# The last two output tiles stored whole, one by ScalarE and one by SP

## The chip, the cores and the metric

The kernel runs on one core of one Trainium2 chip. The metric is the device time of one execution in microseconds (us), as the median of several runs. A profiled execution comes with a trace: its span runs from the first to the last instruction, and all times in the rows below are microseconds from the start of that span. In the rows PE is TensorE (PEld its weight loads), DVE is VectorE, ACT is ScalarE, POOL is GpSimd and SP is SyncE. A "q" behind an engine's name (SPq, ACTq) is its instruction queue: the issue of a transfer, a branch or a wait.

## The reference, cut to what matters

The first half is a gated linear attention (an mLSTM) over 4 batches, 8 heads, 768 steps and 40 values per head. Its output, reordered to 3072 tokens of 320 values, goes through a feed-forward layer of width 2048 with a rational activation:

```python
x = attn_out.transpose(0, 2, 1, 3).reshape(B * S, H * D)   # 3072 x 320
h = x @ w_in
P = a[0] + a[1] * h + a[2] * h**2 + a[3] * h**3
Q = 1.0 + abs(b[0]) * abs(h) + abs(b[1]) * h**2
out = (P / (Q + 1e-06)) @ w_out                            # 3072 x 320
```

The change concerns how the last rows of `out` leave the chip, and nothing of the computation.

## The kernel before, in words

A flag computed at the start selects one of two copies of the whole program (`tc.If` and `Else`); the profiled execution ran the first. Behind the selected copy each engine takes a branch (line 328) past the other copy, to a common ending (line 1479) in which SP waits for the transfers' semaphores and the engines meet.

The attention produces token blocks; the feed-forward layer takes them in 12 steps of 256 tokens, numbered 0 to 11. Each step has eight chunks of the hidden width and collects its result in two PSUM tiles of 128 tokens by 320 values, `po`. At its end the operation `ev` (`f_ev`) copies each of them to an SBUF tile, `ot` (128 partitions of 320 float32, 160 KB), and `ed` (`f_ed`) stores it to `out`. The 128 partitions of a tile are 64 steps of one batch and the same 64 steps of the next batch, and the batches lie 768 rows apart in `out`. So a store of the first kind writes 64 partitions (80 KB) to 64 consecutive rows, and a tile takes two such stores.

All engine work stands in one list, `ORDER`, written out by hand; the operations are recorded in that order, and each engine keeps it. In it `ed` is an operation on SP for all tiles but the very last. The last step, 11, has the tiles `ot11_0` and `ot11_1`. ScalarE evicts the first and VectorE the second, at about the same time. The two stores of `ot11_0` are issued by SP (operation `ed_11_7`). The two stores of `ot11_1` are issued from inside `f_ev`, the first by ScalarE's queue and the second by SP:

```python
if engine == "DVE" and not split:
    f_ed(t, (nc.scalar, nc.sync))
```

As line 30 (`_Queue`) hands out `dma_start` of any queue but SP's unwrapped, ScalarE's store carries its own line number (L1360) in the trace, and those of SP carry that of the helper, L34.

Of the kernel before, what the change touches and what calls it, by code (L numbers as in the profile page):

```python
# [314 lines left out]
whalf_11_7.1 m_11_6 rm_11_6 gl_11_5 p1half_11_7.1 p3half_11_7.1 f3_11_4 f3_11_4.1 f2_11_5 f2_11_5.1 yhalf_11_7  # L315
r0half_11_7 ghhalf_11_7 mhalf_11_7 rmhalf_11_7 f3_11_5 f3_11_5.1 f2_11_6 f2_11_6.1 gl_11_6 f3_11_6 f3_11_6.1
yhalf_11_7.1 r0half_11_7.1 ghhalf_11_7.1 mhalf_11_7.1 rmhalf_11_7.1 glhalf_11_7 glhalf_11_7.1 f2half_11_7
f2half_11_7.1 f3half_11_7 f3half_11_7.1 ev_11_7 ed_11_7 ev_11_7.1
"""


# [69 lines left out]
def _program(  # L391
# [16 lines left out]
    nc = _Ordered(tc)  # L408
    B, H, S, D = q.shape
    DM, DFF = w_in.shape  # L410
    P = 128
    L = 64
# [47 lines left out]
    def ring(pool, tag, shape, name, dt=F32, at=None):  # L460
        k = plan.slot[tag] if at is None else at
        return pool.tile(shape, dt, tag=f"{tag}{k}", name=name, bufs=1)
# [759 lines left out]
    def feed_forward(n, i):  # L1222
        d = {}
        size = SIZES[n]
        split = n < SPLIT
# [3 lines left out]
        last = n == len(SIZES) - 1 and i >= NS - HALVED  # L1229
# [77 lines left out]
        def parts_of(t):  # L1307
            return [(t, 0, 0, DM)] if t < 8 - BANKS else [(0, DM, 0, 512 - DM), (1, DM, 512 - DM, DM)]
# [28 lines left out]
        def f_ev(t, engine):  # L1337
            ot = d["ot", t] = ring(fp, "ot", [P, DM], f"ot{n}_{t}")
            for b, at, lo, hi in parts_of(t):
                to, po = ot[:, lo:hi], PO[n, half][b][:, at : at + hi - lo]  # L1340
                if split:
                    nc.vector.scalar_tensor_tensor(
                        to, po, pa[:, 3:4] if square else 1.0, PT[n][:, t, lo:hi], op0=ALU.mult, op1=ALU.add
                    )
                elif engine == "DVE":
                    nc.vector.tensor_scalar(to, po, pa[:, 3:4] if square else 1.0, None, op0=ALU.mult)
                elif square:
                    nc.scalar.activation(to, po, AF.Copy, scale=pa[:, 3:4])
                else:
                    nc.scalar.copy(to, po)  # L1350
            if engine == "DVE" and not split:
                f_ed(t, (nc.scalar, nc.sync))

        def f_ed(t, queues):
            m = firsts_of[n] + t // 2
            blk, b = divmod(2 * m, B)
            at = blk * P + t % 2 * L
            for j, queue in enumerate(queues):
                rows = out.rearrange("(b s) e -> b s e", b=B)[b + j, at : at + L]
                queue.dma_start(rows, d["ot", t][j * L : (j + 1) * L])  # L1360

        k = f"{n}_{i}"
        a0, a1 = (ps[:, 0:1], ps[:, 1:2]) if square else (pa[:, 0:1], pa[:, 1:2])
# [1 line left out]
        def add(name, engine, cost, fn, r=(), w=(), new=(), part=None, **kw):  # L1365

            def own(x):
                if x not in ("h", "ha", "w", "p", "gH", "gL"):
                    return x
                if part is None or not last:  # L1370
                    return f"{x}{k}"
                return f"h{k}p{part}" if x == "h" else f"{x}{k}.{part}"

            plan.add(
                f"{name}{'half' if last and part is not None else ''}_{k}", engine, cost, fn,
                [own(x) for x in r], [*(own(x) for x in w), f"turn {name}"],
                [(own(x).split(".")[0], t) for x, t in new], **kw,
            )
# [39 lines left out]
        if i == NS - 1:  # L1418
            for t in range(groups):
                o = f"ot{n}_{t}"  # L1420
                e = "DVE" if split or t == groups - 1 and n == len(SIZES) - 1 else "ACT"
                add("ev", e, 0.32, lambda t=t, e=e: f_ev(t, e), r=[f"pt{n}.{t}"] if split else [],
                    w=[*(po[b] for b, *_ in parts_of(t)), o], new=[(o, ("ot", BUFS["ot"]))], lag=2.5)
                if e == "ACT" or split:
                    add("ed", "SP", 0.6, lambda t=t: f_ed(t, (nc.sync, nc.sync)), r=[o], lag=2.5)

    stg = ctx.enter_context(tc.tile_pool(name="stage", bufs=2))
# [18 lines left out]
    for n, i in steps + [(n, i) for n in range(SPLIT, len(SIZES)) for i in range(NS)]:  # L1446
        feed_forward(n, i)
# [36 lines left out]
```

## Time and profile before

| | |
|---|---|
| device time, 3 runs | 499.54, 499.55 and 501.44 us; median 499.55 us |
| the profiled execution's own time | 500.97 us |
| its span, first to last instruction | 499.1 us |
| what lies outside the span | 1.9 us |
| mean granted TensorE clock | 0.993 |
| TensorE busy | 479.0 us (96% of the span) |
| last matmul ends, last eviction ends | 491.5 us, 492.1 us |

The profiled execution is 1.4 us above the median of the runs, so differences worked out on the span are laid on the median. The change is confined to what follows 491.9 us: the last 7 us of the span, in which no engine computes.

### The profile page before, as it was taken

How to read it: one execution, taken by the hardware profiler on the slowest of the kernel's cores; microseconds unless marked ns; L12 is line 12 of the kernel's file. 1: busy time of each engine (PE TensorE's matmuls, PEld its weight loads, DVE VectorE, ACT ScalarE, POOL GpSimd, SP SyncE). 2: the span in 40 equal slices, each digit the busy share in tenths (PEclk: the TensorE clock that was granted, in tenths of full speed). 3: DMA queues.
4: the chain of work that ended last, by engine and by line, in shares of the span. 5: the costliest groups of instructions: out<-in, count | busy, mean ns of one | idle time of the engine just before them, and what ended most of it. 6: DMA issues, size and time to landing. Idle time of an engine off the chain costs nothing.

```text
span 499.1 us, 14216 instructions
## 1 busy us (share of the span) xinstructions
PE 479.0 (96%) x5631; PEld 460.3 (92%) x5631; DVE 415.7 (83%) x696; ACT 402.6 (81%) x701; POOL 394.6 (79%) x392
## 2 busy tenths in 40 slices
PE   4899999999999999999999999999999999999993
PEld 4789989899999999999999999999999999999993
DVE  6789899999889788997788977888887788868793
ACT  1779999879977587879886888997778788778981
POOL 3789899888796888888889787888677877887772
PEclk9999999999999999999999999999999999999998
DMA  7979965157444343731541330504241040010101
GB/s 195 230 149 250 303 148 106 36 97 139 102 88 87 73 73 62 150 83 24 100 101 43 67 72 1 110 1 102 65 107 18 2 88 1 1 30 2 26 1 34
DMA packets 119837, 42.01 MB, mean 84 GB/s; under 512 B 104274, under 2 KB 112530, under 8 KB 119762
## 3 DMA queue, kind: packets, MB, share of 16 engines
q1 hardware_dynamic: 118626, 40.77, 37.4%
q8 instruction: 46, 0.75, 0.7%
q10 hardware_dynamic: 1136, 0.25, 0.3%
q14 instruction: 29, 0.24, 0.2%
HBM read 36.90 MB, written 4.10 MB: 82 GB/s over the span
## 4 chain that ended last, share of the span: by engine, by line
PE 75%; DVE 7%; POOL 4%; ACT 4%; issue 3%; DMA 1%; POOLq 0%; DVEq 0%
PE ph L34 31%; PE po L34 29%; PE y L34 4%; PE kq L34 4%; PE ow L34 3%; PE ps L34 2%; DVE w L34 2%; DMA qn<-in_q_dram 1%; PE px L34 1%; DVE gH L34 1%; PE hot L34 1%; POOL p L34 1%; DVE gL L34 1%; POOL w L34 1%; POOL wi L34 1%
## 5 line engine op out<-in xcount | busy, mean ns | idle before, releaser
L34 POOL TENSOR_TENSOR p<-p,w 128x512 f32<-128x512 f32 (+1 forms) x97 | 131.1, 1352 | 61.1 <-DVE w L34 58.3
L34 PE MATMUL ph<-xk,wi 128*128 128x256 f32 x1152 | 169.4, 283 | 1.7 <-DVE xk L34 0.8
L34 PEld LDWEIGHTS ph<-xk,wi 128*128 128x128 f32 x1152 | 148.1, 188 | 3.9 <-DVE xk L34 1.0
L34 PE MATMUL po<-wo,gH 128*128 128x320 f32 x768 | 133.4, 310 | 0.0
L34 POOL TENSOR_TENSOR w<-w,ha 128x512 f32<-128x512 f32 (+1 forms) x97 | 127.1, 1313 | 6.4 <-ACT w L34 3.2
L34 PEld LDWEIGHTS po<-wo,gH 128*128 128x128 f32 x768 | 115.6, 188 | 0.7
L34 DVE SCALAR_TENSOR_TENSOR gL<-p,ps,ph 128x512 fp32r<-128x512 f32 (+1 forms) x97 | 71.1, 734 | 21.5 <-POOL p L34 19.8
L34 DVE SCALAR_TENSOR_TENSOR w<-w,gH 128x512 f32<-128x512 f32 (+1 forms) x97 | 83.9, 865 | 3.9
L34 ACT ACTIVATE ph<-w,cd 128x512 f32<-128x512 f32 (+1 forms) x97 | 66.5, 686 | 21.4 <-DVE p L34 11.0
L34 ACT ACTIVATE w<-ha,ba 128x512 f32<-128x512 f32 (+1 forms) x97 | 78.6, 811 | 5.5 <-POOL p L34 2.1
L34 DVE SCALAR_TENSOR_TENSOR gH<-p,ps,ph 128x512 fp32r<-128x512 f32 (+1 forms) x97 | 71.4, 736 | 13.3 <-ACT ph L34 7.4
L34 PE MATMUL po<-wo,gL 128*128 128x320 f32 x384 | 77.2, 314 | 0.8 <-DVE gL L34 0.6
L34 PE MATMUL ph<-xk,wj 128*128 128x256 f32 x384 | 75.2, 277 | 0.0
L34 DVE SCALAR_TENSOR_TENSOR p<-p,ps,ph 128x512 f32<-128x512 f32 (+1 forms) x97 | 70.2, 732 | 4.7 <-ACT p L34 3.6
L34 ACT ACTIVATE ha<-ph 128x512 f32<-128x512 f32 (+1 forms) x97 | 57.3, 591 | 15.5 <-PE ph L34 15.1
L34 ACT ACTIVATE p<-ph,ps 128x512 f32<-128x512 f32 (+1 forms) x97 | 65.3, 678 | 4.1 <-DVE gL L34 3.6
L34 PEld LDWEIGHTS po<-wo,gL 128*128 128x128 f32 x384 | 59.0, 188 | 3.1 <-DVE gL L34 2.3
L34 PEld LDWEIGHTS ph<-xk,wj 128*128 128x128 f32 x384 | 58.0, 188 | 0.0
L34 ACT ACTIVATE ph<-ph 128x512 f32<-128x512 f32 (+1 forms) x97 | 56.0, 578 | 2.1
L34 PE MATMUL hot<-ident 128*128 128x128 f32 x180 | 25.6, 293 | 4.0 <-DVE flag_out L386 4.0
L34 PEld LDWEIGHTS hot<-ident 128*128 128x128 f32 x180 | 23.3, 205 | 4.5 <-issue 4.0
L34 DVE TENSOR_TENSOR pm<-ps,e 128x256 f32<-128x256 f32 x48 | 18.6, 418 | 9.1 <-PE ps L34 8.8
(133 smaller groups left out, 605.7 us busy)
## 6 DMA issues: line engine op xcount, KB each, us to landing
rawo<-in_moe_w_out_dram SPq DMA_DIRECT2D x8, 640.0 KB, 7.7
ab<-scrA SPq DMA_DIRECT2D x40, 128.0 KB, 3.4
rawi<-in_moe_w_in_dram SPq DMA_DIRECT2D x8, 512.0 KB, 6.7
kr<-in_k_dram SPq DMA_DIRECT2D x24, 160.0 KB, 3.5
qn<-in_q_dram SPq DMA_DIRECT2D x24, 160.0 KB, 3.6
og<-in_o_gate_dram SPq DMA_DIRECT2D x48, 80.0 KB, 3.3
out_dram<-ot SPq DMA_DIRECT2D x47, 80.0 KB, 2.3
vb<-in_v_dram SPq DMA_DIRECT2D x46, 80.0 KB, 3.1
```

Of the source, the lines that this page charges most:

```text
L34: made = fn(*args, **kwargs)
```

## The change

The two stores of each of the last two tiles become one store of 128 partitions. Its destination is an access pattern of three levels: 2 batches, 64 rows in each, 320 values. ScalarE's queue issues that of `ot11_0`, which it evicted itself, and SP that of `ot11_1`, which VectorE evicted. Both are issued from inside `f_ev`, so the operation `ed_11_7` leaves the list. All other tiles are stored as before.

```diff
@@ ORDER, its end
-f2half_11_7.1 f3half_11_7 f3half_11_7.1 ev_11_7 ed_11_7 ev_11_7.1
+f2half_11_7.1 f3half_11_7 f3half_11_7.1 ev_11_7 ev_11_7.1
@@ f_ev
-            if engine == "DVE" and not split:
-                f_ed(t, (nc.scalar, nc.sync))
+            if last and not split:
+                f_ed(t, (nc.scalar if engine == "ACT" else nc.sync,))
@@ f_ed
-            for j, queue in enumerate(queues):
-                rows = out.rearrange("(b s) e -> b s e", b=B)[b + j, at : at + L]
-                queue.dma_start(rows, d["ot", t][j * L : (j + 1) * L])
+            rows = out.rearrange("(b s) e -> b s e", b=B)[b : b + 2, at : at + L]
+            if len(queues) == 1:
+                queues[0].dma_start(rows, d["ot", t])
+            else:
+                for j, queue in enumerate(queues):
+                    queue.dma_start(rows[j], d["ot", t][j * L : (j + 1) * L])
@@ feed_forward
-                if e == "ACT" or split:
+                if split or not last:
                     add("ed", "SP", 0.6, lambda t=t: f_ed(t, (nc.sync, nc.sync)), r=[o], lag=2.5)
```

SP's instructions at the end of the executed copy, before the change; a row names the destination, the source, the destination's shape from the slowest level to the fastest, and the semaphores waited for (DMAHW is that of an earlier transfer):

```order
L34 DMA out_dram<-ot_1_7407 64x320 [waits DMAHW0_49,Activation_49]
L34 DMA out_dram<-ot_1_7407 64x320 [waits DMAHW1_49]
L34 DMA out_dram<-ot_0_7673 64x320 [waits DMAHW2_49,Activation_49]
L34 DMA out_dram<-ot_0_7673 64x320 [waits DMAHW4_49]
L34 DMA out_dram<-ot_1_7677 64x320 [waits DMAHW5_49,DVE_49]
L328 UNCONDITIONAL_BRANCH
```

The same place after it:

```order
L34 DMA out_dram<-ot_1_7407 64x320 [waits DMAHW0_49,Activation_49]
L34 DMA out_dram<-ot_1_7407 64x320 [waits DMAHW1_49]
L34 DMA out_dram<-ot_1_7676 2x64x320 [waits DMAHW3_49,DVE_49]
L328 UNCONDITIONAL_BRANCH
```

Three stores of 64x320 have become one of 2x64x320, which waits for VectorE's eviction; the stores of step 10 above it stand as they did.

ScalarE's last instructions before the change:

```order
L34 ACTIVATE ph_7_1_7589<-ph_7_1_7589 128x256 [waits Activation_49]
L34 ACTIVATE ot_0_7673<-po_0_0_7419,pa 128x320 [waits DMAHW7_49,DMAHW6_49,PE_49]
L1360 DMA out_dram<-ot_1_7677 64x320 [waits DVE_49]
L328 UNCONDITIONAL_BRANCH
```

And after it:

```order
L34 ACTIVATE ph_7_1_7589<-ph_7_1_7589 128x256 [waits Activation_49]
L34 ACTIVATE ot_0_7673<-po_0_0_7419,pa 128x320 [waits DMAHW7_49,DMAHW6_49,PE_49]
L1360 DMA out_dram<-ot_0_7673 2x64x320 [waits Activation_49]
L328 UNCONDITIONAL_BRANCH
```

ScalarE still issues one store; it now waits for its own eviction in place of VectorE's. No other row of any engine has moved, in either copy of the program.

## Rows read from the trace of the kernel before

**Rows 1.** The page: span, and busy time of the engines.
```profile
span 499.1 us, 14216 instructions
PE 479.0 (96%) x5631; PEld 460.3 (92%) x5631; DVE 415.7 (83%) x696; ACT 402.6 (81%) x701; POOL 394.6 (79%) x392
```

**Rows 2.** The timeline from 491.3 us to the end: start, duration, instruction.
```profile
490.94 0.57 PE L34 MATMUL po<-wo,gL 128*128 128x320 f32 x2
491.40 0.53 ACT L34 ACTIVATE ot<-po,pa 128x320 f32<-128x320 f32 x1 [3.45 <-PE po L34]
491.55 0.55 DVE L34 TENSOR_SCALAR ot<-po,pa 128x320 f32<-128x320 f32 x1 [0.66 <-PE po L34]
491.95 2.60 SPq L34 DMA_DIRECT2D out_dram<-ot  x3
492.13 0.55 ACTq L1360 DMA_DIRECT2D out_dram<-ot  x1
```

**Rows 3.** SP's three last issues, apart: duration in ns, and time to landing.
```profile
L34 SPq DMA_DIRECT2D out_dram<-ot x1: 467/467/467, 492.0 to 492.0; - x1
DMA to landing us min/median/max: 2.6/2.6/2.6
...
L34 SPq DMA_DIRECT2D out_dram<-ot x1: 1348/1348/1348, 492.5 to 492.5; - x1
DMA to landing us min/median/max: 2.9/2.9/2.9
...
L34 SPq DMA_DIRECT2D out_dram<-ot x1: 637/637/637, 493.9 to 493.9; - x1
DMA to landing us min/median/max: 3.7/3.7/3.7
```

**Rows 4.** The branch to the ending: duration in ns, first and last start.
```profile
L328 ACTq COMPARE_BRANCH  x1: 38/38/38, 492.7 to 492.7; - x1
L328 SPq COMPARE_BRANCH  x1: 46/46/46, 494.6 to 494.6; - x1
```

**Rows 5.** The ending itself, columns as before; the last row of 497.9 to 498.2 us.
```profile
L1479 SPq EVENT_SEMAPHORE  x10: 17/28/28, 497.7 to 499.0; - x10
L1479 DVEq DRAIN  x2: 10/26/41, 495.1 to 498.6; - x2
L1479 ACTq DRAIN  x2: 8/38/67, 495.6 to 498.6; - x2
...
L1479 SPq EVENT_SEMAPHORE  x6: 28/28/28, 497.9 to 498.2; - x6
```

**Rows 6.** Transfers, 492 to 499.1 us: busy tenths of 16 engines in 40 slices.
```profile
DMA  0002108979720179158960010010000000000100
```

**Rows 7.** Queues, 495.06 to 496.51 us, then 496.49 to 497.06: packets, MB, share.
```profile
q8 instruction: 1, 0.02, 6.2%
...
DMA  6000000006000000006000000000600000000000
q1 hardware_dynamic: 5, 0.01, 6.7%
```

**Rows 8.** Transfers, 1.6 to 1.7 us, and the first issue of the span.
```profile
q1 hardware_dynamic: 2, 0.00, 1.0%
...
flag_a<-in_moe_a_dram SPq DMA_DIRECT2D x1, 0.0 KB
```

**Rows 9.** Transfers, 494.08 to 494.26 us: the rest of ScalarE's store.
```profile
DMA packets 7, 0.01 MB, mean 43 GB/s; under 512 B 1, under 2 KB 7, under 8 KB 7
q10 hardware_dynamic: 7, 0.01, 11.9%
```

**Rows 10.** Transfers, 468 to 472 us: four stores of step 10.
```profile
DMA packets 320, 0.33 MB, mean 82 GB/s; under 512 B 64, under 2 KB 320, under 8 KB 320
q1 hardware_dynamic: 320, 0.33, 38.2%
```

## The prediction, made before the changed kernel ran

> **What bounds the kernel now.** The page comes first: TensorE is busy 96% of a span of 499.1 us [rows 1]. The change touches nothing before 491.9 us, so only the end matters. The timeline shows that the two evictions end at 491.93 (ScalarE) and 492.10 (VectorE), and that nothing but four issues of stores follows [rows 2]. Yet the span goes on for 7.0 us, and the views of single lines tell with what.
>
> SP issues three stores one after another: 0.47, 1.35 and 0.64 us long, the last from 493.91 to 494.55 [rows 3]. Then it branches at 494.6 [rows 4], and its first instruction in the ending starts at 497.7, 3.1 us later [rows 5]. ScalarE's way is alike: branch at 492.7, ending at 495.6. So a jump costs an engine about 3 us here, and SP jumps last. From SP's first wait in the ending to the end of the span it is another 1.4 us [rows 5].
>
> The last store lands 3.7 us after 493.91, at 497.6 [rows 3], just before SP begins to wait. That is late by its own measure: its last engine sent four packets between 496.5 and 497.04, when the rest was done, and right before them a block of 16 KB of instructions had held one engine: 6.2% of 16 engines over 1.45 us, so 1.4 us [rows 7]. Two things thus end almost together: SP's own way (issue, jump, waits), which decides, and the landing of the last store, just ahead of SP's first wait.
>
> **The change, part by part.** One store costs an issuer one issue whatever its rows, if the issues behind these rows are a guide: the four here move the same 80 KB in 0.47 to 1.35 us. I take 0.55 us, ScalarE's [rows 2]; 1.35, met where SP and ScalarE issued together, is the other end.
>
> *SP's way.* Two of its three issues go. Its one store waits for VectorE's eviction, as ScalarE's did, and so starts at 492.13 [rows 2]. It ends between 492.6 and 493.5, in place of 494.55: SP reaches its jump 1.05 to 1.95 us earlier, and its first wait at 495.8 to 496.7. Nothing is queued behind this issue but the jump.
>
> *ScalarE's way.* Its store waits for its own eviction and starts at 491.95, when SP's first did. Its jump comes 0.2 us earlier, which gains nothing: it was in the ending 2 us ahead of SP [rows 5].
>
> *The transfers.* This is where the sum is decided: the bytes are the same, 256 rows of 1280 bytes, but over how many of the 16 engines? A store of 64 rows leaves 80 packets: 64 rows, and 16 small ones that report completion, one for each engine (four stores: 320 packets, 64 of them under 512 bytes [rows 10]). The one transfer in the program whose slowest level is 1, the flag's single row, leaves 2 packets, one of data and one of completion [rows 8]: it used one engine. So the shape decides the count. Every other transfer here has 16 or a multiple of 16 as its slowest level on both sides; the new stores are the first with a slowest level of 2, by the order's rows (2x64x320). I take it that the slowest level is what is dealt out, and that each new store runs on two engines, 64 rows on each. The trace has no transfer with a 2 in that place, so this is inference between two ends: 2 engines, or 16 as for the stores before.
>
> The Trainium skill states the rule by which this would happen, in "DMA: Bandwidth & Descriptors", section "Why a DMA increments its semaphore by 16 and not by 1": the engines of a transfer are the largest number up to 16 that divides the slowest level other than 1 on both sides, and they are the lowest-numbered ones. For 128 partitions against 2 batches it gives 2, and the same two for both stores. The trace agrees as far as its single-row transfer goes (one completion packet); no run so far shows a 2.
>
> *The price on two engines.* If both stores are dealt out from the same first engine, each of the two has 128 rows to send. For a row's price the nearest stretch is the one in which two late engines alone finish ScalarE's store: 7 packets, one of them small, in 11.9% of 16 engines over 0.18 us [rows 9], 0.34 us for 6 rows, or 57 ns a row. The other ends are 95 ns with all 16 engines at work (38.2% of 16 engines over 4 us for 256 rows [rows 10]) and some 140 ns for the last engine after the block of instructions (four rows in 0.55 us [rows 7]). Two engines that are otherwise alone are the case of the first. 128 x 57 ns is 7.3 us. That both take the same pair is a choice too: no row tells which engine is which, but nothing in the two issues differs that could part them. Separate pairs are priced with the rivals.
>
> *The sum.* ScalarE's issue ends at 492.50; after SP's first issue ended at 492.42 the first packets of stores came with the seventh of the 40 slices, from 493.07 on, 0.65 us later (the digits before it are instructions) [rows 6]. So packets run from 493.15 to 500.45. A last packet reported 0.5 us after it left (497.04 to 497.6 [rows 3, 7]): 500.95. SP has been waiting since 496.7 at the latest; when its wait for these stores is released, the rest of its list and the ending remain, 1.2 us by the row from 497.9 to the end [rows 5] (1.0 to 1.4). The span ends at 502.15, 3.05 us later than before. The gain on SP's way is swallowed whole: it is 4 us ahead of the landing. On the profiled execution that is 504.0 us, on the median 499.55 + 3.05 = **502.6 us**.
>
> **The rivals.**
>
> *Sixteen engines, so faster.* If rows are dealt out by their total, 128, each engine has 16 rows for both stores: at 95 ns that is 1.5 us, and all has landed by 495.4 even if SP's issue takes 1.35 us. SP first asks at 495.8. Then its shorter way is the whole result: 1.05 to 1.95 us less, 497.6 to 498.5 us. For it speaks that every store so far used 16 engines; against it, that all of those had a slowest level of 64. The point from which it decides: what lands by 497.9 costs nothing against before, so an engine may spend 4.2 us on its rows, 74 of them at 57 ns. 256 rows need at least four engines for that.
>
> The Trainium skill also advises this very step, in "DMA: Bandwidth & Descriptors", section "Rules for kernel authors": two transfers to disjoint halves of the partitions gain nothing, and one of 128 partitions is to be used. By that alone the result would be this rival's. Its reason is that both halves use all 16 engines anyway, which rows 10 agree with for the stores of before.
>
> *Two engines at the loaded price, so slower by more.* Two queues would feed the same two engines, which no stretch of the trace shows. At 95 ns, 128 rows take 12.2 us, and the time is 499.55 + 8.0 = 507.5 us; at 140 ns it is 513. For it speaks that single late engine; against it the stretch of rows 9, where two late engines were quick.
>
> *Two engines, and a block of instructions on one of them.* Every jump fetches instructions over the same 16 engines. A block that falls on one of the two adds up to its 1.4 us: 504.0 us. Of the four last stores ScalarE's [rows 9] and SP's last [rows 7] ended on late engines, so this is no rarity.
>
> *Two separate pairs, so no change.* With 64 rows an engine, 3.65 us from 493.3 to 494.1 on, the later store lands between 497.5 and 498.3 and the span ends 1.2 us behind that: 0.4 us less to 0.4 us more, 499.1 to 500.0 us. Rows 9 fit it as well as they fit one pair.
>
> **How the numbers follow.** One pair near 57 ns a row gets 0.52, one pair at a higher price or behind instructions 0.23, sixteen engines (or at least four a store) 0.20, two pairs 0.05. The prediction is the first: 502.6 us, by itself 502.0 to 506.0 with the dearer rows and the fetched blocks counted in. The range for all has to reach into the sixteen-engine case, 497.6 to 498.5; from 497.8 to 505.5 it leaves out a little of that case and about half of the dear one, some 0.17. Half a per cent, 2.5 us, is about what a measurement here tells from no change. Slower by more than it: nearly all of the dear case and 0.44 of the first's 0.52, as the sum stands only 0.55 us above the bound: 0.66. Faster by more than it would need more than SP's 1.95 us: 0.03. The rest is 0.31.
>
> **What would show it.** Right: the landing time of the two new stores, the later of them about 8.8 us after its issue in place of 2.6 to 3.7; 64 data packets and two completions for each; the share of 16 engines near an eighth from 493.2 to 500.5; SP's jump at 492.7 to 493.5 and its wait afterwards. If landing is 3 us or less with 16 completions each, the engine count was wrong and the time falls to some 498 us. If two engines are seen but rows start 95 ns apart or more, the price was. If the ending begins later than the landing, the jump was.

## The result, and the profile after

The changed kernel takes 504.62 us (median of 6 runs, 503.81 to 505.21) against 499.6 us before (6 runs, 498.96 to 501.44): 1.0095 times the time, 95% interval 1.0077 to 1.0113, or 5.0 us more between the medians. The profiled execution took 505.07 us.

The page says nothing about the cause: the engines' busy times are those of before within 0.3 us, and only the span is 4.1 us longer. The timeline from the last eviction on (start, duration, instruction) answers to [rows 2]:

```profile
span 503.2 us, 14213 instructions
...
491.29 0.53 ACT L34 ACTIVATE ot<-po,pa 128x320 f32<-128x320 f32 x1 [3.44 <-PE po L34]
491.44 0.55 DVE L34 TENSOR_SCALAR ot<-po,pa 128x320 f32<-128x320 f32 x1 [0.66 <-PE po L34]
491.85 1.13 ACTq L1360 DMA_DIRECT2D out_dram<-ot  x1
492.02 0.64 SPq L34 DMA_DIRECT2D out_dram<-ot  x1
```

Everything up to here stands where it stood: the last eviction ends at 492.0, in place of 492.1. From there the span went on for 7.0 us before and goes on for 11.2 us now. The branches and the ending (duration in ns, first and last start; the two SPq rows of the ending cover 495 to 500.4 and 500.4 to 503.2 us) answer to [rows 4, 5]:

```profile
L328 SPq COMPARE_BRANCH  x1: 46/46/46, 492.7 to 492.7; - x1
L328 ACTq COMPARE_BRANCH  x1: 38/38/38, 493.0 to 493.0; - x1
...
L1482 SPq EVENT_SEMAPHORE  x2: 17/22/28, 495.5 to 495.6; - x2
L1482 SPq EVENT_SEMAPHORE  x8: 17/28/28, 500.6 to 503.1; - x8
...
L1482 ACTq DRAIN  x2: 8/39/70, 499.0 to 502.7; - x2
```

SP jumps 1.9 us earlier than before and is in the ending at 495.5, 2.2 us earlier. It clears two waits and then stands still until 500.6 (another of the same row is released only at 502.1). What it waits for are the two new stores. Their queues (packets, MB, share of 16 engines) from 493 to 502 us, and in three parts of that stretch (493.1 to 495.2, 498 to 500 and 500.2 to 501.1 us):

```profile
DMA packets 266, 0.39 MB, mean 43 GB/s; under 512 B 4, under 2 KB 260, under 8 KB 260
q10 hardware_dynamic: 130, 0.16, 6.8%
q1 hardware_dynamic: 130, 0.16, 4.9%
...
q10 hardware_dynamic: 47, 0.06, 12.7%
...
q1 hardware_dynamic: 40, 0.05, 6.9%
q10 hardware_dynamic: 37, 0.05, 6.2%
...
q1 hardware_dynamic: 34, 0.04, 13.0%
```

Each store left 130 packets: 128 rows and two small ones. So each ran on two engines, where a store of 64 rows left 80 packets, 16 of them small [rows 10]. From 498 to 500 us no block of instructions passes, and both queues together hold 6.9 + 6.2%, about an eighth of 16 engines. From 500.2 to 501.1, when ScalarE's rows are all out, SP's queue holds 13.0% alone and passes 34 rows in 0.9 us, about as many a microsecond as both queues together before. So it is one pair for both stores: with a pair of its own, SP's store would not have gone faster when ScalarE's was done. The pair is full until 501.1; one of its engines has rows until 501.5. The 77 packets from 498 to 500 are 76 rows and a small one, which is about 52 ns a row on each engine. The row of 47 packets is the first 2.1 us, 89 ns a row with the pair just as busy, and all of them are ScalarE's: the first row of SP's store left at 495.28, 2.6 us after its issue ended.

Between the slow beginning and 498 us there is a second slow stretch. From 496.1 to 496.9 us the queues passed:

```profile
q10 hardware_dynamic: 7, 0.01, 9.2%
q1 hardware_dynamic: 8, 0.01, 3.4%
```

These are 15 rows in 0.8 us, or 107 ns a row. Over the whole of 495.2 to 498 us it was 83 rows, 67 ns each.

### The profile page after: what moved, and what is told of

It reads as the page before. It is cut to its first block, busy times and chain, and to the rows that moved or that the text cites. A ratio compares the mean times of both kernels' runs of the same rounds, so it can differ in the third digit from the quotient of the medians.

```text
span 503.2 us, 14213 instructions
## 1 busy us (share of the span) xinstructions
PE 479.1 (95%) x5631; PEld 460.4 (91%) x5631; DVE 415.4 (83%) x696; ACT 402.5 (80%) x701; POOL 394.7 (78%) x392
## 4 chain that ended last, share of the span: by engine, by line
PE 79%; ACT 6%; DVE 4%; issue 2%; DMA 2%; SPq 2%; POOL 2%; DVEq 0%; ACTq 0%; POOLq 0%
PE ph L34 32%; PE po L34 29%; PE y L34 5%; PE kq L34 4%; PE ow L34 3%; PE ps L34 3%; PE hot L34 2%; SPq L34 2%; PE px L34 1%; DMA rawi<-in_moe_w_in_dram 1%; ACT ph L34 1%; DMA gate_f<-in_i_gate_dram 1%; DVE w L34 1%; ACT w L34 1%; ACT ha L34 1%
```

## The experiments

All were compared with the kernel before on the same chip, whose medians there were 499.5 to 499.8 us. "The tail" is the time from the end of the last eviction to the end of the span in the profiled execution: 7.0 us before, 11.2 us changed.

**One store of 128 partitions, without the level of 2.** Each store writes 128 consecutive rows:

```diff
             if len(queues) == 1:
+                at = blk * P
+                rows = out.rearrange("(b s) e -> b s e", b=B)[b + t, at : at + 2 * L]
                 queues[0].dma_start(rows, d["ot", t])
```

> As the changed kernel, but each of the two stores writes its 128 partitions to 128 consecutive rows, so that the destination has two levels (128 x 320) and no level of 2; two half tiles end up in each other's rows of the output. Theory A (the level of 2 confines a store to two engines, and the 128 rows that each of the two must send are the loss): both stores use all 16 engines, 144 packets each, landing 2.5 to 3.5 us after their issue; only SP's shorter way to its jump is left, 497.7 to 498.6 us. Rival B (a store of 128 partitions is itself slow to land, or its issue from ScalarE's queue is, whatever its destination): some 504 us again.

Measured: 497.94 us, 0.9970 times before (0.9955 to 0.9986), tail 4.9 us. The timeline, SP's jump and ending, and the queues from 491.8 to 494 us:

```profile
491.02 0.36 ACTq L1362 DMA_DIRECT2D out_dram<-ot  x1
491.19 0.37 SPq L34 DMA_DIRECT2D out_dram<-ot  x1
...
L328 SPq COMPARE_BRANCH  x1: 46/46/46, 491.6 to 491.6; - x1
L1484 SPq EVENT_SEMAPHORE  x10: 17/28/28, 494.7 to 496.0; - x10
...
q10 hardware_dynamic: 144, 0.16, 23.8%
q1 hardware_dynamic: 144, 0.16, 22.2%
```

The same bytes, issuers and number of stores, and with 16 small packets each they take two microseconds in place of eight. B falls: neither 128 partitions nor ScalarE's queue is slow. What is left is SP's shorter way, and the ten waits run through without a stop. As the rows land where the reference does not want them, this version only parts the theories.

**The slowest level set to 8 and to 4.** The stores take interleaved groups of 16 or 32 rows, `c` groups each:

```diff
             if len(queues) == 1:
+                at = b * S + blk * P
+                rows = out[at : at + 4 * L].rearrange("(c g s) e -> g c s e", c=8, g=2)[t]
                 queues[0].dma_start(rows, d["ot", t])
```

> As the changed kernel, but each of the two stores has a slowest level of 8 in its destination (8 groups of 16 rows, 32 rows apart, the two stores interleaved in 256 consecutive rows; the output's last 128 rows stay unwritten and 128 others are overwritten). Theory A (the slowest level is dealt out): 8 engines, so 128 + 8 packets a store and 32 rows an engine for both, landed by 496 and hidden behind SP's way; 497.7 to 498.6 us. Rival H (2 is special, anything else goes to 16 engines): 144 packets a store, the same time. Only the packets tell these two apart.

> The same with a slowest level of 4 (4 groups of 32 rows, 64 rows apart; the same rows left unwritten and overwritten). Theory A: 4 engines, 128 + 4 packets a store, 64 rows an engine for both stores: at 52 ns and with up to 1.5 us of instruction blocks the last row leaves 3.3 to 4.8 us after the first, and the time is 498.5 to 500.5 us, about the point from which the engine count decides. Rival H: 144 packets a store, 497.7 to 498.6 us.

Measured: 500.71 us for both, 1.0023 (1.0012 to 1.0033) with 8 and 1.0030 (1.0015 to 1.0045) with 4. The queues, and SP's jump and ending, with 8:

```profile
q10 hardware_dynamic: 136, 0.16, 15.3%
q1 hardware_dynamic: 136, 0.16, 13.0%
...
L328 SPq COMPARE_BRANCH  x1: 46/46/46, 491.8 to 491.8; - x1
L1484 SPq EVENT_SEMAPHORE  x10: 17/28/28, 496.9 to 498.2; - x10
```

And with 4:

```profile
q10 hardware_dynamic: 132, 0.16, 12.4%
q1 hardware_dynamic: 132, 0.16, 9.4%
...
L328 SPq COMPARE_BRANCH  x1: 46/46/46, 491.8 to 491.8; - x1
L1484 SPq EVENT_SEMAPHORE  x10: 17/28/28, 494.6 to 498.5; - x10
```

128 + 8 and 128 + 4 packets: the engine count is the slowest level, and H falls. The times are a miss, above all with 8. There all rows had gone out by 494.9, and SP jumped 0.8 us after the last eviction, where it was 2.5 us before; but the jump took 5.1 us in place of 3.1, and the gain was used up. With 4 the jump took 2.8 us, and SP then waited for the rows. Why the jump was long with 8 is taken up at the end.

**Half of the change.** Only ScalarE's tile is stored with the level of 2:

```diff
-                f_ed(t, (nc.scalar if engine == "ACT" else nc.sync,))
+                f_ed(t, (nc.scalar,) if engine == "ACT" else (nc.sync, nc.sync))
```

> Only the tile that ScalarE evicts is stored with the level of 2, by ScalarE; VectorE's tile goes out in two stores of 64 rows from SP. Theory A: each of the two engines has 64 + 8 rows in place of 128; at the 52 to 57 ns a row and the 1 to 1.7 us of instruction blocks seen in the changed kernel the last row leaves between 497 and 499, and the time is 499.3 to 501.0 us, close to before. Rival D (each store with the level of 2 costs a fixed amount, whatever else shares its engines): half the change's loss, about 502 us.

Measured: 501.39 us, 1.0046 (1.0030 to 1.0062), tail 8.4 us: 0.4 us above A's bound and 0.6 us under D's value, so this time does not part them cleanly. The trace shows the sharing, though. The landing of SP's second ordinary store, its queue from 494.5 to 496.3 us, and from 491.8 to 492.8 us:

```profile
out_dram<-ot SPq DMA_DIRECT2D x1, 80.0 KB, 6.1
...
q1 hardware_dynamic: 10, 0.01, 3.0%
...
q1 hardware_dynamic: 17, 0.01, 21.3%
```

It landed 6.1 us after its issue, where such stores took 2.6 to 3.7 [rows 3]. The ten packets are its last eight rows and two of its sixteen completions; all others were out by 494.4. That is four rows on each of two engines, held up among the other store's rows, which a fixed cost of D's kind does not explain. The last line bears on the slow beginning: SP's queue alone kept 21.3% of 16 engines busy, more than three, with 10 rows and 7 small packets in a whole microsecond. So rows were slow at that time on other engines than the pair, too.

**One of the two stores alone.** ScalarE's store stays, VectorE's tile is not stored:

```diff
-            if last and not split:
-                f_ed(t, (nc.scalar if engine == "ACT" else nc.sync,))
+            if last and engine == "ACT":
+                f_ed(t, (nc.scalar,))
```

> The changed kernel without the store of VectorE's tile (its 128 rows of the output stay unwritten): ScalarE's store with the level of 2 runs alone. Theory K (rows are held up for some 2.1 us after a store's first row, while its descriptors are still being made, and follow each other at 52 ns behind that): long rows and gaps in the first 2.1 us alone, 25 to 28 rows an engine in them, then 52 ns a row, 4.0 to 4.3 us from the first row to the last. Rival L (the long rows come from two queues on one engine): none, 64 x 52 ns = 3.3 to 3.5 us.

Measured, in a single execution: 501.19 us, 1.4 us above the median before, tail 7.8 us. The queue over the whole store (492.7 to 498.2 us), in its first 2.6 us, and from 495.3 to 496.9 us:

```profile
q10 hardware_dynamic: 130, 0.16, 10.5%
...
q10 hardware_dynamic: 62, 0.08, 12.9%
...
q10 hardware_dynamic: 56, 0.07, 11.9%
q8 instruction: 1, 0.02, 3.7%
```

62 rows in 2.6 us are 84 ns a row, 55 rows and a small packet in 1.6 us are 58 ns. The whole took 4.9 us, more than K's 4.3, because the end was slow too. L (3.5 us at most) falls: one queue alone has the slow beginning.

**Both stores from one queue.** SP issues both:

```diff
-                f_ed(t, (nc.scalar if engine == "ACT" else nc.sync,))
+                f_ed(t, (nc.sync,))
```

> The changed kernel with both stores issued by SP, one behind the other, in place of one each by ScalarE and SP. Theory K: the rows of the first store are held up as before and those of the second once more; 8.0 to 8.6 us from the first row to the last, 504 to 505.5 us. Rival L (two queues in turn on one engine): one queue has no long rows, 6.7 to 7.0 us and 503 us or less. If SP's second issue is held up until the first store's descriptors are made, its jump is late, but still hidden behind the rows.

Measured: 504.8 us, 1.0112 (1.0076 to 1.0147), tail 10.9 us. Its queue from 492.2 to 500.6 us, and from 492.2 to 495 us:

```profile
q1 hardware_dynamic: 260, 0.33, 12.2%
...
q1 hardware_dynamic: 64, 0.08, 12.8%
```

256 rows in 8.3 us again, so which queues feed the pair does not matter. The first 2.8 us passed 64 rows at 88 ns; the other 192 needed 5.5 us, 57 ns a row. K named the total, but its reason is not confirmed: the rows of the second store began at about 496.6 and went at 57 ns a row from there to 498.6, so they had no slow beginning of the first one's kind.

**No jump at the end.** Only the copy of the program that the flag selects is built, so that no engine branches past another and no instructions are fetched for it; the kernel no longer serves the other inputs:

```diff
-        with tc.If(flag > 0) as test:
-            _program(tc, True, common, *args)
-        with test.Else():
-            _program(tc, False, common, *args)
+        _program(tc, True, common, *args)
```

> The changed kernel with only the copy of the program that the flag selects, without the branch past the other one at the end (the kernel no longer serves inputs that select the other copy; its start changes too, so that only the end is to be compared). Theory E (the instruction blocks that the jumps fetch fall on the two engines of the stores and hold their rows up): without jumps no such blocks, and the last row leaves 6.6 to 7.0 us after the first, in place of 8.3. Rival G (two queues in turn on one engine make a row dearer than the 52 ns at which rows follow each other): 8 us or more again. From the last eviction to the end of the span: E 9.5 us, G 11 us, against 11.2 us with the jump.

> The kernel before, with one copy of the program and no branch in the same way. If SP's way with its jump of 3.1 us decided the end, as the prediction has it, the end is now decided by the landing of the last store, some 1.6 us after its issue ends, and from the last eviction to the end of the span it is 5 to 5.6 us in place of 7.0. If the landing decided already: 6.5 us or more.

Measured: 504.09 us with the change (1.0084, 1.0058 to 1.0110, tail 10.7 us) and 497.84 us without it (0.9967, 0.9952 to 0.9982, tail 4.2 us). With the change, the queues from 493 to 502 us, in the first 2.2 us of rows, and from 496.1 to 497.2 us:

```profile
DMA packets 260, 0.33 MB, mean 36 GB/s; under 512 B 4, under 2 KB 260, under 8 KB 260
q10 hardware_dynamic: 130, 0.16, 6.8%
q1 hardware_dynamic: 130, 0.16, 4.9%
...
q10 hardware_dynamic: 52, 0.07, 12.8%
...
q10 hardware_dynamic: 11, 0.01, 9.4%
q1 hardware_dynamic: 11, 0.01, 3.4%
```

Not one block of instructions is among the packets, and the rows still took 8.0 us, 0.3 us less than with the jump. E falls, but for those 0.3 us: the rows are slow in their first 2.2 us (85 ns) and again from 496.1 to 497.2 (100 ns) without any help from instructions. Without the change, the span, the last eviction and the landing of SP's three stores:

```profile
core 0 of [0], span 497.1 us
...
492.37 0.55 DVE L34 TENSOR_SCALAR ot<-po,pa 128x320 f32<-128x320 f32 x1 [0.66 <-PE po L34]
...
DMA to landing us min/median/max: 2.0/2.1/2.2
```

The stores land 2.0 to 2.2 us after their issue, and the tail is 2.8 us shorter than with the jump, more than expected. So the end of the kernel before waited for the jump and what comes with it. This run takes two things away at once, the jump and the fetched blocks, one of which passed right before the last rows to land [rows 7]. In the kernel before the last landing and the jump ended 0.1 us apart, so the share of each is not parted.

**Two versions that keep 16 engines and two issues or fewer for SP.** The first leaves four stores of 64 rows but gives each issuer its own tile; the second evicts both tiles into one SBUF tile and stores 64 partitions of both halves to the 128 rows of one batch, one store per issuer:

```diff
-                f_ed(t, (nc.scalar if engine == "ACT" else nc.sync,))
+                f_ed(t, (nc.scalar if engine == "ACT" else nc.sync,) * 2)
```

```diff
...
+            if last and t == 1:
...
+                for j, queue in enumerate((nc.scalar, nc.sync)):
+                    rows = out.rearrange("(b s) e -> b s e", b=B)[b + j, blk * P : (blk + 1) * P]
+                    queue.dma_start(rows.rearrange("(t s) e -> s t e", t=2), PT["end"][j * L : (j + 1) * L])
...
```

> Four stores of 64 rows as before the change, but each issuer stores the tile it follows: ScalarE both halves of its own, SP both halves of VectorE's. Theory A: 16 engines throughout, everything lands by 496; SP has two issues in place of three and reaches its jump 0.2 to 1.4 us earlier, 498.2 to 499.4 us. Rival C (SP's issues never decided the end before the change, the landing of the last store did): the time follows the last landing, within 0.3 us of before unless a block of instructions holds an engine.

> Both evictions write one SBUF tile of two halves, and each of the two stores takes 64 partitions of both halves to the 128 rows of one batch: the same rows as the reference wants, one store per issuer, 160 KB each, slowest level 64 on both sides, then 2, then 320. Theory A: 16 engines, 144 packets a store, landing in 2.5 to 3.5 us, and the whole of SP's gain, 497.7 to 498.6 us. Rival B (two stores of 160 KB are slow in themselves, or three levels are): 502 us or more.

Measured: 500.18 us (1.0007, 0.9994 to 1.0019, tail 6.5 us) and 499.3 us (0.9995, 0.9984 to 1.0007, tail 6.3 us). Both are misses: no difference from before that the runs can tell. Of the second, the issues and SP's jump and ending:

```profile
491.68 0.62 SPq L34 DMA_DIRECT2D out_dram<-ptend  x1
491.70 0.67 ACTq L1361 DMA_DIRECT2D out_dram<-ptend  x1
...
L328 SPq COMPARE_BRANCH  x1: 46/46/46, 492.3 to 492.3; - x1
L1492 SPq EVENT_SEMAPHORE  x10: 17/28/28, 496.6 to 497.8; - x10
...
out_dram<-ptend SPq DMA_DIRECT2D x1, 160.0 KB, 2.9
out_dram<-ptend ACTq DMA_DIRECT2D x1, 160.0 KB, 3.7
```

The stores land in 2.9 and 3.7 us, so B falls here too. SP jumps 0.7 us after the last eviction, where it was 2.5 us before; but the jump took 4.2 us. In the first version SP's two issues took 0.47 and 1.25 us beside ScalarE's two, and its jump 3.3 us. Its last store landed some 0.9 us ahead of SP's first wait (497.6), so by this trace SP's way decided and not, as rival C has it, the landing. No version that keeps both copies of the program and writes the right rows was faster than the kernel before.

## Why the prediction held, and where its sum was short

**The two engines: right.** This was the step that was inference, and it held to the packet: 128 rows and two completions a store. (The prediction's list of signs has 64 data packets for each store; that is the number on each engine, as its own sum has it.) Levels of 4 and 8 gave 4 and 8, 128 and 64 gave 16. By the rule of the Trainium skill ("DMA: Bandwidth & Descriptors", section "Why a DMA increments its semaphore by 16 and not by 1"), the number of engines is the largest up to 16 that divides the slowest level on both sides. These runs agree with it in every case that they have. The advice of the Trainium skill on the same page (section "Rules for kernel authors"), one transfer of 128 partitions in place of two halves, held where the destination was 128 consecutive rows (497.94 us) and not where its slowest level was 2 (504.62 us).

**One pair for both: right.** Both queues together held about an eighth of 16 engines, and SP's queue held as much by itself when ScalarE's was done. No row had decided this, and the choice came out.

**The rival with 16 engines: right in its size once out of two.** 497.6 to 498.5 us was its price, and 497.94 us the measurement with two plain stores of 128 rows. The two stores of both halves, on 16 engines as well and with the right rows, took 499.3 us, as SP's jump took 4.2 us there and not the 3 us counted on.

**The price of a row: the term that was too small.** The prediction took 57 ns for each of 128 rows, 7.3 us. It was 65 ns on the whole, 8.3 us from the first row (493.14) to the last (501.47). From 498 on it was 52 ns, better than assumed. The loss against that pace is about half in the first 2.1 us (89 ns) and most of the rest between 495.2 and 498 (67 ns). It does not come from instruction blocks (all but 0.3 us of it is there without them), nor from two queues in turn (as slow with one queue or one store). What makes rows slow stays open. The dearer row accounts for the 1.0 us by which the span grew more than the predicted 3.05 us, and for most of what the later store took longer: SP's wait for it was released 10.1 us after its issue began, in place of 8.8. The rival with a block of instructions was priced at 504.0 us; that it stands nearest to the measured 504.62 us is chance, as the runs put the blocks at 0.3 us.

**What surrounds it: right, the start by luck.** The first row left at 493.14 (493.15 predicted), though ScalarE's issue took 1.13 us and not 0.55. The prediction counted 0.65 us from the end of an issue; here the row left 0.16 us after it, and the two differences nearly cancel. Counted from the start of the issue, it was 1.12 us before and 1.29 us now. From the last row to the end of the span it was 1.7 us, as predicted (0.5 + 1.2).

**From the span to the median: 0.9 us.** The difference of the spans is 4.1 us, that of the medians 5.0. The profiled execution before lay 1.4 us above its median and that after 0.45 us above its own; the prediction laid a difference of single executions on the median as if they were alike. With the 1.0 us of the rows this is the whole of the 2.0 us by which the measured median lies above 502.6 us.

**SP's way: right before, too simple after.** That the end before waited for SP's jump and the blocks it fetches, the tail without them shows (4.2 us in place of 7.0). That a shorter way is gained whole as soon as the rows land in time was wrong: the point of decision, four engines, was given with a jump of 3 us, and with 8 engines the jump took 5.1 us.

## What to carry to other kernels

Before merging stores, look at the slowest level of both sides as the instruction has them: here a store of 128 partitions whose destination steps over 2 batches outermost ran on two engines, and the completion packets of the profile (64 + 16, 128 + 2) show the count at once. At the end of this program nothing hid such stores, so 256 rows on one pair cost 8 us where 16 engines took 2. Count the jump of the last issuer there as well: one issue in place of three gained 1.6 us where the jump stayed at 3.1 us, and nothing where it grew to 4.2 or 5.1 us.

## What had not been expected

A jump's length is not fixed. ScalarE's, 2.9 us before [rows 4, 5], took 6.0 us in the changed kernel (493.0 to 499.0) and 5.9 us with half the change; SP's ran from 2.7 to 5.1 us. The long ones occur only beside stores on few engines or stores of two tiles at once. With a level of 8 both engines had jumped by 492.1, and no block of instructions left from 491.8 to 494.2; the blocks came when most rows were out. That the fetched blocks stand behind rows on the same engines would explain it, but the trace does not say on which engine a block ran, so this is argued and not shown.

On ScalarE an issue costs more with a short outermost level: it needed 1.12 to 1.21 us for a store with a slowest level of 2, 4 or 8 in each of six kernels, 0.55 us for 64 x 320 before (0.57 and 0.98 us for two in a row), and 0.36 us for 128 x 320. On SP the difference is smaller: 0.55 to 0.72 us for such a store, 0.37 us for 128 x 320, and from 0.47 us up for 64 x 320.

The end of the last eviction, with the same program ahead of it, lay between 490.2 and 492.4 us in the profiled executions of the kernels with both copies. So only tails are compared and not the times at which they end. Each tail is that of one execution, and as no spread of them was measured, half a microsecond between two of them is not taken to decide anything.
